# A fused per-channel scale and 384x384 matmul: reordering the first loads and splitting one weight copy

## The chip, the cores and the metric

The kernel runs on one core of one Trainium2 chip. The metric is the device time of one execution in microseconds (us); the median of three runs of the kernel before is 574.29 us (574.18 to 574.39). The core has a matrix engine (TensorE, PE in the profile; its weight loads have a row of their own, PEld), a vector engine (VectorE, DVE), a scalar engine (ScalarE, ACT), GpSimd (POOL) and SyncE (SP), which only issues DMAs and waits. SyncE and ScalarE each have a DMA queue of their own (q1 and q10 in the profile). The engines run independently and wait for each other through semaphores.

## The reference

```python
# x: (1, 384, 384, 384) bf16, dw: (1, 1, 384) bf16, pw: (384, 384) bf16
out = x * dw[0, 0][None, None, None, :]            # k = 1: the depthwise convolution is a scale per channel
return jnp.einsum('bhwc,cd->bhwd', out, pw)        # 147,456 rows of 384 times a 384 x 384 matrix
```

The scale can be moved into the matrix once, `w = dw[:, None] * pw`, and then the work is `x @ w`: 147,456 rows in 288 supertiles of 512 rows.

## The kernel before

TensorE contracts over partitions, but x arrives with its rows on partitions. VectorE therefore transposes x in 32x32 blocks of 32-bit words (pairs of bf16 channels), and TensorE works with contractions of 32 rows, four of them side by side in the array. The matrix must have the matching order of rows and copies in all four groups of 32 partitions. Making it is the *prologue*: TensorE multiplies a scaled selection matrix with pw into PSUM, six *pieces* `i = 2k + r` (k: 128 rows of pw, r: even or odd channels), and ScalarE or VectorE copies each piece from PSUM to `w_r`. Then the main loop runs: transposes on VectorE, 48 matmuls per supertile on TensorE, one PSUM copy per supertile on ScalarE, loads and stores by DMA.

The loads at the start (x0 and x1 are the first two chunks of x, of 384 KB each; x2 is 768 KB):

```python
w_eng = [1, 0, 1, 1, 1, 1]            # piece -> engine: 1 = ScalarE, 0 = VectorE
w_all = [(s_wr[e], w_eng.count(e)) for e in range(2)]      # what GpSimd awaits before its copy of w_r

nc.scalar.dma_start(dw_row[:], ...).then_inc(s_dw, 16)                  # L178
nc.sync.dma_start(pw_n[:, 0], pw[0:P, :]).then_inc(s_pw, 16)            # L179
nc.sync.dma_start(pw_n[:, 1:3], pw[P:C, :]....).then_inc(s_pw2, 16)     # L180
load_x(0)                                                               # L133, SyncE
# ... SyncE then issues x1, x2, x3, ... and later the stores
```

TensorE's prologue and the start of the main loop:

```python
w_first = {(0, 0): [(0, 1), (1, 3)], (4, 0): [(1, 4)], (4, 1): [(1, 5)]}   # step -> (engine, copies) awaited
steps = [(b, par) for b in range(4) for par in range(2)] + [(4, 0), (5, 0), (4, 1), (5, 1)]

idle_work(4)                     # L242: 4 x 4 matmuls of ones, results never read
nc.tensor.wait_ge(s_dw, 16)
...                              # L255: dw turned onto partitions by 3 matmuls
idle_work(2)                     # L242: 2 x 4 more
nc.tensor.wait_ge(s_pw, 16)
times = {(2, 0): 2, (2, 1): 2}   # these two pieces are computed twice (the same result)
for k in range(3):
    if k == 1:
        nc.tensor.wait_ge(s_pw2, 16)
    nc.tensor.wait_ge(s_sw, k + 1)                 # VectorE has scaled selection matrix k
    for r in range(2):
        if k == 2:
            nc.tensor.wait_ge(*w_done[r])          # the PSUM banks of piece r are free again
        for v in [0, 1] * times.get((k, r), 1):
            mm = nc.tensor.matmul(PS[(k + 1) % 2][:, 2 * r + v, :D], ...)   # L275
        mm.then_inc(s_w)
# main loop, first supertile, first step (b, par) = (0, 0): waits for s_t[0][0] (x0's first block is
# transposed) and for w_first[(0, 0)]; then 4 matmuls (L225), next step, ...
```

VectorE and ScalarE:

```python
def transposes(t, j):
    ...
    for h in range(2):
        if h == 0 and j == 0:
            nc.vector.wait_ge(sem, n)              # the chunk of x has landed
        if h == 0 and jj == 0:
            for b in range(3):                     # x0's first half in three blocks
                x_b = Xw[:, :, 0, 32 * b : 32 * b + 32]
                nc.vector.transpose(out=Tw[:, b], in_=x_b).then_inc(s_tb if b else s_t[0][0])   # L367
            continue
        ...                                        # L369: all other transposes, half a supertile each

def w_out(i):
    e, k, r = w_eng[i], i // 2, i % 2
    out, in_ = w_r[:, 2 * k : 2 * k + 2, r, :], w_ps(i)
    o = nc.vector.tensor_copy(out, in_) if e == 0 else nc.scalar.copy(out, in_)     # L385
    o._wait_ge(s_w, i + 1)
    o.then_inc(s_wr[e])
...
for i in range(6):
    w_out(i)
transposes(*order[0])        # x0
transposes(*order[1])        # x1
```

ScalarE executes, in this order: the DMA issue of dw, a table load (L341), two tiny copies (L341), its five pieces, and then one PSUM copy per supertile (L429).

Of the kernel before, what the change touches and what calls it, by code (L numbers as in the profile page):

```python
# [26 lines left out]
def kernel(  # L27
# [12 lines left out]
    nc = tc.nc  # L40
    P = nc.NUM_PARTITIONS
    B, H, W, C = x.shape
# [17 lines left out]
    NT = len(chunks)  # L60
# [13 lines left out]
    pw_n = raw[:, 0 : 3 * D].rearrange("p (k d) -> p k d", d=D)  # L74
# [29 lines left out]
    s_pw = nc.alloc_semaphore("s_pw")  # L104
    s_pw2 = nc.alloc_semaphore("s_pw2")
# [5 lines left out]
    s_wr = [nc.alloc_semaphore(f"s_wr{e}") for e in range(2)]  # L111

    with tc.tile_critical(sync_engine=mybir.EngineType.Pool, no_gpsimd_drain=True):
        def x_of(t):
            g, i, off, first, L = chunks[t]
            if first + 2 == NS:
                return Xl[:], s_xl, 32
            n = sum(len(ls) > i for ls in groups[g % NR : g + 1 : NR])
            return Xs[g % NR][:, 4 * off : 4 * (off + L), :], s_x[g % NR][i], 16 * n

        def load_x(t, eng=nc.sync):
            g, i, off, first, L = chunks[t]
            dst, sem, _ = x_of(t)
            rows = xf[512 * first : 512 * (first + L), :]
            if first + 3 < NS:
                src = rows.rearrange("(p s) c -> p (s c)", p=P)
                dst = dst.rearrange("p s c -> p (s c)")
                if i == 0 and g >= NR:
                    je = g_end[g - NR]
                    eng.wait_ge(s_t[je % 2][1], je // 2 + 1)  # L130
            else:
                src = rows.rearrange("(a k q) c -> q a k c", k=4, q=4)
            eng.dma_start(dst, src).then_inc(sem, 16)  # L133
# [39 lines left out]
            eng.dma_start(dst, src).then_inc(s_o[g % NR], 16)  # L173

        w_eng = [1, 0, 1, 1, 1, 1]
        w_all = [(s_wr[e], w_eng.count(e)) for e in range(2)]

        nc.scalar.dma_start(dw_row[:], dw.rearrange("a e c -> a (e c)")).then_inc(s_dw, 16)  # L178
        nc.sync.dma_start(pw_n[:, 0], pw[0:P, :]).then_inc(s_pw, 16)  # L179
        nc.sync.dma_start(pw_n[:, 1:3], pw[P:C, :].rearrange("(k p) d -> p k d", p=P)).then_inc(s_pw2, 16)  # L180
        load_x(0)

        todo = []
        for t, (g, i, off, first, L) in enumerate(chunks):
            if 0 < t < NT - 2:
                todo.append((g_end[g - NR] if g >= NR else -1, load_x, (t,)))
            for k in range(n_parts[t] - (first + 1 == NS)):
                todo.append((first + L * (k + 1) // n_parts[t] + 1, store, (t, k)))
# [15 lines left out]

        w_done = [(s_wr[e], w_eng[: i + 1].count(e)) for i, e in enumerate(w_eng)]

        w_first = {(0, 0): [(0, 1), (1, 3)], (4, 0): [(1, 4)], (4, 1): [(1, 5)]}

        def w_ps(i):
            return PS[0 if i in (2, 3) else 1][:, 2 * (i % 2) : 2 * (i % 2) + 2, :D]  # L210
# [28 lines left out]
        def idle_work(n):  # L239
            for _ in range(n):  # L240
                for i in range(4):
                    nc.tensor.matmul(  # L242
                        PS[0][:, 2 * (i % 2) + i // 2, :D],
                        lhsT=ones[32 * i : 32 * i + 32, 0:P],
                        rhs=ones[32 * i : 32 * i + 32, :],
                        start=True,
                        stop=True,
                        tile_position=(32 * i, 0),
                    )
# [10 lines left out]
                stop=True,  # L260
            )
        mm.then_inc(s_df)
        idle_work(2)
        nc.tensor.wait_ge(s_pw, 16)
        times = {(2, 0): 2, (2, 1): 2}
        for k in range(3):
            if k == 1:
                nc.tensor.wait_ge(s_pw2, 16)
            nc.tensor.wait_ge(s_sw, k + 1)
            for r in range(2):  # L270
                if k == 2:
                    nc.tensor.wait_ge(*w_done[r])

                for v in [0, 1] * times.get((k, r), 1):
                    mm = nc.tensor.matmul(  # L275
                        PS[(k + 1) % 2][:, 2 * r + v, :D],
                        lhsT=sel_w[64 * v : 64 * v + 64, k, r, :, :].rearrange("p q w -> p (q w)"),
                        rhs=pw_n[64 * v : 64 * v + 64, k, :],
                        start=True,
                        stop=True,  # L280
                        tile_position=(64 * v, 0),
                    )
                mm.then_inc(s_w)
# [22 lines left out]
        for m in range(4):  # L306
# [14 lines left out]
            out=eye[:],  # L321
            in_=ones[:, 0:P],
# [20 lines left out]
        def transposes(t, j):  # L343
            g, i, off, first, L = chunks[t]
            jj = first + j
            s = jj % 2
            if jj + 1 == NS:
                nc.vector.wait_ge(s_xk, 32)
                Tw = Ts[s][:].bitcast(U32).rearrange("p b (m w) -> p (b m) w", w=32)
                for v in range(2):  # L350
                    blocks = slice(12 * v, 12 * v + 12)
                    ins = nc.vector.transpose(out=Tw[:, blocks], in_=Xk[:, blocks].bitcast(U32))  # L352
                    ins._wait_ge(s_pe, 2 * (jj - 2) + v + 1)
                    ins.then_inc(s_t[s][v])
                return
            X, sem, n = x_of(t)
            Xw = X.bitcast(U32).rearrange("p (k l) c -> p k l c", l=L)
            Tw = Ts[s][:].bitcast(U32).rearrange(
                "p b (k i) -> p b k i" if t < 2 else "p b (i k) -> p b k i", k=4
            )  # L360
            for h in range(2):
                if h == 0 and j == 0:
                    nc.vector.wait_ge(sem, n)
                if h == 0 and jj == 0:
                    for b in range(3):
                        x_b = Xw[:, :, 0, 32 * b : 32 * b + 32]
                        nc.vector.transpose(out=Tw[:, b], in_=x_b).then_inc(s_tb if b else s_t[0][0])  # L367
                    continue
                ins = nc.vector.transpose(  # L369
                    out=Tw[:, 3 * h : 3 * h + 3],  # L370
                    in_=Xw[:, :, j, 96 * h : 96 * h + 96].rearrange("p k (b w) -> p b k w", w=32),
                )
                if jj >= 2:
                    ins._wait_ge(s_pe, 2 * (jj - 2) + h + 1)
                ins.then_inc(s_t[s][h])
# [3 lines left out]

        order = [(t, j) for t in range(NT) for j in range(chunks[t][4])]  # L380

        def w_out(i):
            e, k, r = w_eng[i], i // 2, i % 2
            out, in_ = w_r[:, 2 * k : 2 * k + 2, r, :], w_ps(i)
            o = nc.vector.tensor_copy(out, in_) if e == 0 else nc.scalar.copy(out, in_)  # L385
            o._wait_ge(s_w, i + 1)
            o.then_inc(s_wr[e])
# [3 lines left out]
            out=sel[:],  # L391
            in_=eye[:].rearrange("p (v w r) -> p r w v", v=2, r=2),
# [10 lines left out]
        for i in range(6):  # L403
            w_out(i)
        transposes(*order[0])
        transposes(*order[1])

        for jj, (t, j) in enumerate(order):
            g, i, off, first, L = chunks[t]
# [28 lines left out]
            if jj + 2 < NS:  # L438
                transposes(*order[jj + 2])
# [30 lines left out]
```

## Time and profile before

| what | value | where it is from |
|---|---|---|
| time, median of three | 574.29 us | the times |
| span of the profiled execution | 572.1 us | the page |
| TensorE busy | 567.4 us (99%) | the page, first part |
| VectorE / ScalarE busy | 508.4 us (89%) / 418.6 us (73%) | the page, first part |
| main-loop matmuls (L225) | 13776, in the chain from 6.31 to 566.55 us | chain of waits |
| first copy of a supertile on ScalarE starts | 8.91 us | timeline |
| moved by DMA | 226.88 MB, mean 397 GB/s | the page, second part |

The page is one execution, taken by the hardware profiler. A line of a group reads: line, engine, operation, what it writes and reads, count, then total busy time, mean duration of one in ns, and the idle time of the engine before such instructions with what ended it. Matmuls are pipelined: a duration is longer than the distance to the next one. The first thing to see in the table is that TensorE is occupied nearly from end to end, and that the whole prologue takes the first 6.3 us of 572.1.

### The profile page before, as it was taken

How to read it: one execution, taken by the hardware profiler on the slowest of the kernel's cores; microseconds unless marked ns; L12 is line 12 of the kernel's file. 1: busy time of each engine (PE TensorE's matmuls, PEld its weight loads, DVE VectorE, ACT ScalarE, POOL GpSimd, SP SyncE). 2: the span in 40 equal slices, each digit the busy share in tenths (PEclk: the TensorE clock that was granted, in tenths of full speed). 3: DMA queues.
4: the chain of work that ended last, by engine and by line, in shares of the span. 5: the costliest groups of instructions: out<-in, count | busy, mean ns of one | idle time of the engine just before them, and what ended most of it. 6: DMA issues, size and time to landing. Idle time of an engine off the chain costs nothing.

```text
span 572.1 us, 29707 instructions
## 1 busy us (share of the span) xinstructions
PE 567.4 (99%) x13843; PEld 354.3 (62%) x13843; DVE 508.4 (89%) x588; ACT 418.6 (73%) x298; POOL 13.9 (2%) x41
## 2 busy tenths in 40 slices
PE   9999999999999999999999999999999999999997
PEld 4666666666666666666666666666666666666664
DVE  6899999999999999999999999999999999999996
ACT  6777777777777777777777777777777777777775
POOL 2042000000000000000000000000000000000000
PEclk9999999999999999999999999999999999999999
DMA  8999999999999999999999999999999999997777
GB/s 328 445 395 411 423 416 430 442 417 417 426 413 423 383 398 438 385 387 399 433 380 388 414 415 402 408 405 415 408 395 433 395 391 403 423 389 313 327 287 263
DMA packets 26740, 226.88 MB, mean 397 GB/s; under 512 B 1385, under 2 KB 7274, under 8 KB 22890
## 3 DMA queue, kind: packets, MB, share of 16 engines
q1 hardware_dynamic: 25796, 225.91, 97.5%
q10 hardware_dynamic: 934, 0.89, 0.4%
q14 instruction: 9, 0.07, 0.0%
q8 instruction: 1, 0.02, 0.0%
HBM read 113.54 MB, written 113.25 MB: 396 GB/s over the span
## 4 chain that ended last, share of the span: by engine, by line
PE 99%; ACT 0%; issue 0%
PE ps L225 98%; PE ps L275 1%; PE ps L242 0%; PE ps L310 0%; PE ps L298 0%; ACT O L424 0%; PE ps L255 0%
## 5 line engine op out<-in xcount | busy, mean ns | idle before, releaser
L225 PE MATMUL ps<-w_r,T 32*128 32x384 bf16 x13776 | 560.3, 321 | 0.0
L369 DVE STREAM_TRANSPOSE T<-X 128x384 uint32<-128x384 uint32 x571 | 500.4, 879 | 54.8 <-DMA X<-in_x_dram 2.3
L429 ACT CAST O<-ps 128x1536 bf16<-128x1536 f32 x286 | 411.6, 1439 | 147.0 <-PE ps L225 147.0
L225 PEld LDWEIGHTS ps<-w_r,T 32*128 32x128 bf16 x13776 | 351.6, 93 | 209.0 <-issue 0.9
L339 POOL COPY Xk<-Xl 32x256 bf16<-32x256 bf16 x16 | 6.3, 394 | 0.0
L338 POOL COPY Xk<-Xl 32x128 bf16<-32x128 bf16 x16 | 4.6, 287 | 25.6 <-DMA Xl<-in_x_dram 24.7
L385 ACT CAST w_r<-ps 128x768 bf16<-128x768 f32 x5 | 3.6, 818 | 0.8 <-PE ps L275 0.8
L333 POOL COPY raw<-w_r 32x768 bf16<-32x768 bf16 x4 | 3.3, 819 | 6.4 <-ACT w_r L385 6.2
L242 PE MATMUL ps<-const-bfloat16-1.0 32*128 32x384 bf16 x24 | 2.2, 514 | 1.1 <-PEq L454 1.1
L275 PE MATMUL ps<-raw 64*128 64x384 bf16 x16 | 2.9, 513 | 0.1
L341 ACT ACT_TABLE_LOAD x1 | 1.3, 1283 | 1.5 <-PEq L454 1.5
L420 DVE CAST O<-ps 128x384 bf16<-128x384 f32 x2 | 1.0, 553 | 1.4 <-PE ps L225 1.4
L275 PEld LDWEIGHTS ps<-raw 64*128 64x128 bf16 x16 | 0.9, 114 | 2.2 <-DMA raw<-in_pw_dram 1.1
L369 DVE STREAM_TRANSPOSE T<-Xl 128x384 uint32<-128x384 uint32 x2 | 1.8, 882 | 0.2
L390 DVE TENSOR_REDUCE sel<-eye 128x64 f32<-128x128 bf16 x1 | 0.3, 289 | 1.5 <-POOL eye L320 1.5
L352 DVE STREAM_TRANSPOSE T<-Xk 128x384 uint32<-128x384 uint32 x2 | 1.2, 578 | 0.5 <-PE ps L225 0.4
L242 PEld LDWEIGHTS ps<-const-bfloat16-1.0 32*128 32x128 bf16 x24 | 0.7, 117 | 1.4 <-issue 1.4
L310 PE MATMUL ps<-raw,T 128*128 128x384 bf16 x8 | 1.5, 328 | 0.0
L424 ACT CAST O<-ps 128x384 bf16<-128x384 f32 x2 | 1.0, 479 | 0.7 <-PE ps L310 0.7
L385 DVE CAST w_r<-ps 128x768 bf16<-128x768 f32 x1 | 1.0, 957 | 0.5 <-PE ps L275 0.5
L367 DVE STREAM_TRANSPOSE T<-X 128x128 uint32<-128x128 uint32 x3 | 0.7, 284 | 0.6 <-DMA X<-in_x_dram 0.6
L424 DVE CAST O<-ps 128x384 bf16<-128x384 f32 x2 | 1.1, 558 | 0.1
(14 smaller groups left out, 5.3 us busy)
## 6 DMA issues: line engine op xcount, KB each, us to landing
X<-in_x_dram SPq DMA_DIRECT2D x26, 3840.0 KB, 21.7
out_dram<-O SPq DMA_DIRECT2D x26, 3840.0 KB, 27.6
X<-in_x_dram SPq DMA_DIRECT2D x3, 1536.0 KB, 18.4
out_dram<-O SPq DMA_DIRECT2D x4, 768.0 KB, 7.7
out_dram<-O SPq DMA_DIRECT2D x2, 1536.0 KB, 13.4
X<-in_x_dram SPq DMA_DIRECT2D x1, 2304.0 KB, 20.1
out_dram<-O SPq DMA_DIRECT2D x1, 2304.0 KB, 11.0
X<-in_x_dram SPq DMA_DIRECT2D x4, 384.0 KB, 4.4
```

The source lines that it names most:

```text
L225: mm = nc.tensor.matmul(PS[s][:, q, :D], lhsT=Ts[s][32 * q : 32 * q + 32, b, par::2], rhs=w_r[32 * q : 32 * q + 32, b, par, :], start=(b, ...
L242: nc.tensor.matmul(PS[0][:, 2 * (i % 2) + i // 2, :D], lhsT=ones[32 * i : 32 * i + 32, 0:P], rhs=ones[32 * i : 32 * i + 32, :], start=True ...
L275: mm = nc.tensor.matmul(PS[(k + 1) % 2][:, 2 * r + v, :D], lhsT=sel_w[64 * v : 64 * v + 64, k, r, :, :].rearrange("p q w -> p (q w)"), rhs ...
L310: mm = nc.tensor.matmul(PS[1][:, m, :D], lhsT=Tk[:, P * (m + 2) : P * (m + 3), par], rhs=w_k[:, par, :], start=False, stop=par == 1,)
L333: nc.gpsimd.tensor_copy(w_k[quads[n]], w_r[quads[n], n]).then_inc(s_wk)
L338: nc.gpsimd.tensor_copy(Xk[quads[n], g:8:4, :], x_b).then_inc(s_xk)
L339: nc.gpsimd.tensor_copy(Xk[quads[n], 8 + g : 24 : 4, :], Xl[quads[g], :, 64 * n : 64 * n + 64]).then_inc(s_xk)
L341: nc.scalar.copy(warm[:, s : s + 1], nc.const_aps.tensor(0.0, [P, 1], F32)).then_inc(s_a[s])
L369: ins = nc.vector.transpose(out=Tw[:, 3 * h : 3 * h + 3], in_=Xw[:, :, j, 96 * h : 96 * h + 96].rearrange("p k (b w) -> p b k w", w=32),)
L385: o = nc.vector.tensor_copy(out, in_) if e == 0 else nc.scalar.copy(out, in_)
L424: o = (nc.scalar.copy if n % 2 else nc.vector.tensor_copy)(Ov[:, n, j, :], PS[s][:, n, :D])
L429: a = nc.scalar.copy(Ov[:, :, j, :], PS[s][:, :, :D])
```

## The change

It rearranges the first six microseconds. SyncE now loads the first 256 rows of pw in one DMA, then x0, then x2 and so on; ScalarE's queue loads dw, the last 128 rows of pw, and x1. Piece 3 (`k = 1, r = 1`) is copied out of PSUM by both engines: ScalarE takes its first PSUM bank (384 columns), VectorE the second, and VectorE's half stands between the first and the second transposed block of x0. The waits are adapted: the first main step needs two VectorE copies instead of one, and pw's second semaphore is awaited before k = 2 instead of k = 1. The filler work of TensorE moves too: three groups of `idle_work` instead of two before the pieces, and piece 3 is computed twice instead of pieces 4 and 5. Its purpose is to have x0 and the first four pieces ready earlier, so that the main loop can begin earlier.

```diff
-        w_all = [(s_wr[e], w_eng.count(e)) for e in range(2)]
+        w_all = [(s_wr[0], 2), (s_wr[1], 5)]

         nc.scalar.dma_start(dw_row[:], dw.rearrange("a e c -> a (e c)")).then_inc(s_dw, 16)
-        nc.sync.dma_start(pw_n[:, 0], pw[0:P, :]).then_inc(s_pw, 16)
-        nc.sync.dma_start(pw_n[:, 1:3], pw[P:C, :].rearrange("(k p) d -> p k d", p=P)).then_inc(s_pw2, 16)
+        nc.sync.dma_start(pw_n[:, 0:2], pw[0 : 2 * P, :].rearrange("(k p) d -> p k d", p=P)).then_inc(s_pw, 16)
         load_x(0)
+        nc.scalar.dma_start(pw_n[:, 2], pw[2 * P : C, :]).then_inc(s_pw2, 16)
+        load_x(1, nc.scalar)
...
-            if 0 < t < NT - 2:
+            if 1 < t < NT - 2:
...
-        w_first = {(0, 0): [(0, 1), (1, 3)], (4, 0): [(1, 4)], (4, 1): [(1, 5)]}
+        w_first = {(0, 0): [(0, 2), (1, 3)], (4, 0): [(1, 4)], (4, 1): [(1, 5)]}
...
-        idle_work(2)
+        idle_work(3)
         nc.tensor.wait_ge(s_pw, 16)
-        times = {(2, 0): 2, (2, 1): 2}
+        times = {(1, 1): 2}
         for k in range(3):
-            if k == 1:
+            if k == 2:
                 nc.tensor.wait_ge(s_pw2, 16)
...
                         nc.vector.transpose(out=Tw[:, b], in_=x_b).then_inc(s_tb if b else s_t[0][0])
+                        if b == 0:
+                            w_out(3, 1)
...
-        def w_out(i):
+        def w_out(i, bank=0):
             e, k, r = w_eng[i], i // 2, i % 2
             out, in_ = w_r[:, 2 * k : 2 * k + 2, r, :], w_ps(i)
+            if i == 3:
+                out, in_ = out[:, bank], in_[:, bank]
+                e = 1 - bank
```

## The prediction, made before the changed kernel was run

> **What bounds the kernel now.** I read the page's first part, then the chain of waits, then the timelines of TensorE, ScalarE and VectorE for the first 9 us. The page's busy times:
>
> ```profile
> PE 567.4 (99%) x13843; PEld 354.3 (62%) x13843; DVE 508.4 (89%) x588; ACT 418.6 (73%) x298; POOL 13.9 (2%) x41
> ```
>
> The chain of waits in order of time (start, length, what):
>
> ```profile
> 0.80 0.32 issue
> 1.12 1.49 PE ps L242 x15
> ...
> 3.36 1.47 PE ps L275 x8
> 4.83 0.02 issue
> 4.85 1.47 PE ps L275 x8
> 6.31 560.24 PE ps L225 x13175
> 566.55 0.65 PE ps L298 x16
> ```
>
> The reader is to see that TensorE is the chain, and that L225 runs in one piece for 560.24 us without a wait. Nothing the change touches lies inside that piece. So the change can act in one way only: by the moment at which the main loop starts, and by the speed at which its first matmuls run. Everything after, the tail included (some 5.5 us from 566.55 to the span's end at 572.1), shifts with it.
>
> What ends last before the main loop is in the timelines of ScalarE and VectorE (start, length, operation, and in brackets the idle time before it and its releaser):
>
> ```profile
> 3.91 3.61 ACT L385 CAST w_r<-ps 128x768 bf16<-128x768 f32 x5 [0.79 <-PE ps L275]
> ```
>
> ```profile
> 4.23 0.96 DVE L385 CAST w_r<-ps 128x768 bf16<-128x768 f32 x1 [0.48 <-PE ps L275]
> 5.83 0.70 DVE L367 STREAM_TRANSPOSE T<-X 128x128 uint32<-128x128 uint32 x3 [0.65 <-DMA X<-in_x_dram]
> 6.45 1.45 DVE L369 STREAM_TRANSPOSE T<-X 128x384 uint32<-128x384 uint32 x3
> ```
>
> The trace's single instructions refine this. ScalarE's pieces start at 3.906, 4.602, 5.292, 5.983 and 6.674 us, so 0.69 us apart, and the third (piece 3) reports at 6.12. x0's sixteenth and last completion comes at 5.80, the first transposed block starts at 5.83 and reports at 6.15. TensorE passes its wait at 6.15 and its first main matmul starts at 6.253. Two things end within 0.03 us of each other: the copy of piece 3, and x0. Only shortening both helps.
>
> Second observation: the clock. The same shape takes very different times on the page,
>
> ```profile
> L225 PE MATMUL ps<-w_r,T 32*128 32x384 bf16 x13776 | 560.3, 321 | 0.0
> ...
> L242 PE MATMUL ps<-const-bfloat16-1.0 32*128 32x384 bf16 x24 | 2.2, 514 | 1.1 <-PEq L454 1.1
> ```
>
> that is 321 ns in the loop and 514 in the filler. Groups of four start 0.320 us apart up to 7.18 us (6.542, 6.862, 7.182) and 0.1625 us apart from 7.39 on. The trace's clock record goes to full at 7.253. Between 6.253 and 7.253 the main loop ran at half speed, which cost it 0.5 us.
>
> [...] the record shows full clock at 7.253 and half again at 573.866, 566.61 us apart[...].
> [...] ScalarE's Xl load, issued at 24.51 us, has its packets spread from 28.0 to past 32.4 among SyncE's.
> [...]
>
> **The change, part by part.**
> *Loads.* An issue takes SyncE 0.39 to 0.46 us. x0's issue moves from third to second place, from 1.87 to about 1.41 us: 0.46 earlier. But the DMA engines were already moving pw without a hole: packets of 768 bytes (36 ns each) from 1.97 to about 3.45, then x0's from 3.21 on. Before x0 could finish, 288 KB of pw and 384 KB of x0 had to pass; that remains. New is that x1, issued by ScalarE at about 2.0 (after dw, 0.54 us, and pw's rest, 0.42), has packets ready about 0.6 us after its issue ends, near 3.1, and takes turns with x0. Two estimates for x0's landing: if the slow first packets (up to 1.3 us instead of 121 ns) overlap between the queues, x0 is through at 4.9 and lands 0.3 us later, at 5.2 to 5.3; if the engines simply alternate, it is through at 5.7 and lands at about 6.0 to 6.2. I choose 5.6 us, against 5.80 before.
> pw's first 256 rows: sixteen packets per engine instead of eight, 0.29 us later than 2.84, so 3.13. TensorE waited for the scaled selection until 3.23 anyway, so the first piece stays at 3.36.
> *ScalarE.* Two more issues push the table load from 1.54 to about 2.43; it and the tiny copies then end so that piece 0 can start at about 3.93 instead of 3.906. 0.02 us, nearly nothing. Pieces 0 and 2 take 0.69 each; half of piece 3 is a 128x384 copy, 479 ns by the page's row of that shape in the tail. It starts at 5.31 and reports at 5.81 instead of 6.12: 0.31 gained. Pieces 4 and 5 follow some 0.3 earlier and aren't awaited.
> *VectorE.* Piece 1 ends at 5.18 as before. Then x0's first block, which holds the engine for 0.24 us (5.828 to 6.064 between its starts), then the half copy: 558 ns by the same tail shape, then the semaphore. So the loop's wait ends at x0's landing + 0.03 + 0.24 + 0.56 + 0.02 = landing + 0.85, where before it was landing + 0.35. The half copy has been put behind x0 on the path. With landing at 5.60 the wait ends at 6.45, and the first matmul starts 0.10 later, at 6.55: 0.30 later than before. With landing under 5.15 the floor is 6.03, from piece 1's end.
> *TensorE's filler.* One more idle group fills 3.02 to 3.34, which was empty. Piece 3 done twice fills 4.60 to 4.92, mostly empty before. Without doubling, pieces 4 and 5 end at 5.56 instead of 6.11. So TensorE is busy from 1.12 to 5.56 without a hole, and then idle until 6.55, 1.0 us.
>
> **What this makes of the clock.** In the window 0.43 to 3.84, TensorE was busy 1.90 + 0.48 of 3.41 us (70%) and the clock was not released. After the change it is 2.72 (80%). In the window 3.84 to 7.253 it was busy 0.77 + 1.26 + 1.00 (89%), and it was released. After, it would be 1.72 + 0.70 (71%). [...] each of three ways is open:
> A, [...] the loop runs at full speed from 6.55. Before, it had done by 7.253 what full speed does in half of that 1.0 us, as though it had begun at 6.75 at full speed. So -0.20: 574.1.
> B, the clock still comes at 7.253: a start 0.30 later costs half of that, +0.15: 574.4.
> C, [...] the clock comes at 10.67, +0.15 and half of 3.41 more, +1.85: 576.1.
>
> **Rivals.**
> First: x0 arrives earlier by its whole issue gain, 5.34. Then the wait ends at 6.19, near the 6.15 of before, and only the clock decides: in A -0.46, in B +0.02. For it speaks that x0's first packets were slow for reasons that two queues may hide; against it the shared engines.
> Second: x1's interleaving takes x0 to 6.1: start at 7.05, in A +0.30, in B +0.40. C becomes likelier, as the hole grows to 1.5 us.
> Third: the loop is starved later, since x2 moves up and x1 over. VectorE waited for x2 0.82 us (until 8.72) without delaying TensorE: its result was awaited only at about 10.8, and reported at 9.61 and 10.33. With the same bytes in the same time I expect nothing of this.
> Fourth: a busier DMA or engine through the rest. No instruction there changes; it would be zero.
>
> **Range and chances.** I give A 0.5, B 0.2 and C 0.3. A with the uncertainty of x0 spans 573.8 to 574.6, B 574.3 to 574.7, C 575.9 to 576.3; runs of before differ by 0.2. The middle of the mixture is 574.3. The range that should hold it 8 times in 10 is 573.7 to 576.2; the upper side is long because of C. Two per cent are 11.5 us, more than the whole prologue, so faster 0.004, same 0.99, slower 0.006.
>
> **What would show it.** x0's wait on VectorE ending at 5.6; ScalarE's half copy of about 0.48 us ending at 5.8; a half copy of about 0.56 us on VectorE after the first block; the first L225 near 6.55; and the spacing of its groups: 0.16 from the start (A), from 7.25 (B) or only from 10.67 (C). The L225 piece of the chain should be 559.7 us in A, about 560.1 in B, 561.8 in C. I am wrong if x0 lands before 5.2 or after 6.2, if the clock comes at other times than these windows, or if the loop shows waits further on.

## The result and the profile after

The changed kernel takes 576.24 us (median of 6; 575.75 to 578.37) where the kernel before takes 574.23 (median of 6; 573.91 to 574.39). The medians differ by 2.0 us, a third of a per cent; the ratio of the means is 1.0044, 95% interval 1.0027 to 1.0061. All ratios below are of means, to the kernel before on the same chip. The prediction was 574.3 with a range to 576.2; the result lies just above the range. The six executions fall in two groups, four from 575.75 to 576.43 and two at 577.69 and 578.37. The profile below is of the one at 577.69; a second profile, at 576.31, follows among the experiments (e12).

First part of the page of the changed kernel, busy times:

```profile
PE 568.0 (99%) x13845; PEld 409.3 (71%) x13845; DVE 508.5 (88%) x589; ACT 417.9 (73%) x298; POOL 13.9 (2%) x41
```

TensorE's busy time has hardly moved. The loss is idle time, and the chain of waits says where:

```profile
1.94 8.15 DMA X<-in_x_dram
10.09 0.02 issue
10.12 0.59 DVE T L372
10.71 0.14 issue
10.84 559.56 PE ps L226 x13728
570.40 0.65 PE ps L299 x16
```

Before, the chain was TensorE throughout. Now it runs for 8.15 us along one load of x, issued at 1.94: that is x1, on ScalarE's queue. Its sixteen completions come between 6.80 and 10.09 us; before, between 6.09 and 6.73. VectorE transposes its first half, and only then does TensorE go on. From there the rest is as long as it was: 13,728 matmuls are 286 supertiles, one less than the loop's 287.

TensorE's timeline (start, length, then in brackets the idle time and what ended it):

```profile
3.60 1.27 PE L276 MATMUL ps<-raw 64*128 64x384 bf16 x10
5.54 0.50 PE L276 MATMUL ps<-raw 64*128 64x384 bf16 x4 [0.68 <-DMA raw<-in_pw_dram]
6.71 2.13 PE L226 MATMUL ps<-w_r,T 32*128 32x384 bf16 x48 [0.67 <-DVE w_r L391]
10.84 3.56 PE L226 MATMUL ps<-w_r,T 32*128 32x384 bf16 x44 [2.00 <-DVE T L372]
```

The first supertile (x48) runs at 6.71, then there is nothing until 10.84. VectorE and ScalarE in the same stretch:

```profile
5.70 0.31 DVE L368 STREAM_TRANSPOSE T<-X 128x128 uint32<-128x128 uint32 x1 [0.32 <-DMA X<-in_x_dram]
5.94 0.52 DVE L391 CAST w_r<-ps 128x384 bf16<-128x384 f32 x1
6.38 0.48 DVE L368 STREAM_TRANSPOSE T<-X 128x128 uint32<-128x128 uint32 x2
6.79 0.53 DVE L372 STREAM_TRANSPOSE T<-X 128x384 uint32<-128x384 uint32 x1
10.12 2.46 DVE L372 STREAM_TRANSPOSE T<-X 128x384 uint32<-128x384 uint32 x4 [2.79 <-DMA X<-in_x_dram]
```

```profile
4.14 3.29 ACT L391 CAST w_r<-ps 128x768 bf16<-128x768 f32 x5 [0.15 <-PE ps L276]
```

x0's first block starts at 5.70, the half copy follows it, and after x0 VectorE waits 2.79 us for x1. The hole also costs something afterwards. Busy times by stretch (columns: stretch, length, then PE, PEld, DVE, ACT and POOL busy, PEclk, DMA share, GB/s):

```profile
9.00:10.00 1.00, 0.00 (x0) 0.00 (x0) 0.00 (x0) 1.00 (x1) 0.94 (x2) 1.00 1.11 461
10.00:11.00 1.00, 0.16 (x4) 0.15 (x8) 0.88 (x2) 0.33 (x1) 0.94 (x2) 1.00 1.06 449
11.00:12.00 1.00, 1.00 (x20) 0.62 (x16) 1.00 (x3) 0.00 (x0) 0.03 (x1) 0.52 0.95 406
13.00:14.00 1.00, 1.00 (x20) 0.62 (x16) 0.70 (x1) 0.00 (x0) 0.00 (x0) 0.50 1.22 522
14.00:15.00 1.00, 1.00 (x28) 0.62 (x23) 0.30 (x1) 0.30 (x1) 0.00 (x0) 0.77 1.02 428
```

The granted clock (PEclk) falls to one half at 11.04 us and comes back at 14.45, 3.41 us later; the trace's clock record has both moments.

**The sum.** The last matmul starts 3.85 us later than before. The loop starts 0.46 later (6.71 instead of 6.25). The clock was full from 4.21 on, so the 0.50 us that the cold start cost before is saved. The hole is 2.32 us between two matmul starts, less the usual 0.16: 2.16. The 3.41 us at half speed cost half of that, 1.71, for groups of four matmuls start 0.320 us apart there and 0.1625 before and after. 0.46 - 0.50 + 2.16 + 1.71 = 3.83 (3.82 before rounding). Without the fall of the clock it is 2.12. The same four terms (start of the loop, cold start, holes, fall of the clock) are given for every profile in a table below.

### The profile page after: what moved, and what is told of

It is laid out like the page before. It is cut to its first block, busy times and chain, and to the rows that moved or that the text cites. A ratio compares the mean times of both kernels' runs of the same rounds, so it can differ in the third digit from the quotient of the medians.

```text
span 576.0 us, 29711 instructions
## 1 busy us (share of the span) xinstructions
PE 568.0 (99%) x13845; PEld 409.3 (71%) x13845; DVE 508.5 (88%) x589; ACT 417.9 (73%) x298; POOL 13.9 (2%) x41
## 4 chain that ended last, share of the span: by engine, by line
PE 98%; DMA 1%; ACTq 0%; DVE 0%; issue 0%; ACT 0%; POOLq 0%
PE ps L226 97%; DMA X<-in_x_dram 1%; PE ps L311 0%; PE ps L299 0%; DVE T L372 0%; ACTq L178 0%; ACT O L430 0%; ACTq L181 0%; ACTq L471 0%; POOLq L113 0%; POOLq L460 0%
## 5 line engine op out<-in xcount | busy, mean ns | idle before, releaser
L226 PEld LDWEIGHTS ps<-w_r,T 32*128 32x128 bf16 x13776 | 406.6, 93 | 157.8 <-issue 3.4
L391 ACT CAST w_r<-ps 128x768 bf16<-128x768 f32 (+1 forms) x5 | 3.3, 745 | 0.2 <-PE ps L276 0.2
L391 DVE CAST w_r<-ps 128x768 bf16<-128x768 f32 (+1 forms) x2 | 1.5, 738 | 0.7 <-PE ps L276 0.7
```

The source lines that it names most:

```text
L226: mm = nc.tensor.matmul(PS[s][:, q, :D], lhsT=Ts[s][32 * q : 32 * q + 32, b, par::2], rhs=w_r[32 * q : 32 * q + 32, b, par, :], start=(b, ...
```

## The experiments

Theory 1, from the changed kernel's trace: the packets of x1 (3 KB, ScalarE's queue) and of x2 (6 KB, SyncE's queue) take turns, so x1 gets the smaller share of the bytes. By 8.00 us 103 of x1's packets had started and 97 of x2's. Theory 2: the split copy, which starts the loop later, and the holes in TensorE's work before it.

**e1: x1 back on SyncE, the rest as changed.**

```diff
-        load_x(1, nc.scalar)
-            if 1 < t < NT - 2:
+            if 0 < t < NT - 2:
```

> The changed kernel with x1 loaded by SyncE again, between x0 and x2; ScalarE's queue keeps dw and the last third of pw; split, waits and filler as changed. Theory 1 (x1's packets of 3 KB on ScalarE's queue alternate one for one with x2's of 6 KB on SyncE's, so x1 lands at 10.1 us and the second supertile waits 2.0 us): x1 lands before 7, no hole after the first supertile, 574.2 to 574.6. Theory 2 (the split copy, which sets the loop's start to 6.71 us, and the holes in TensorE's work before it are the cost): the start stays near 6.7 and some 1 to 2 us stay lost, 575.2 to 576.

Measured: 574.28 us (573.85 to 575.97, 12 runs), ratio 1.0004 (0.9993 to 1.0016). x1 lands at 7.65. TensorE's timeline:

```profile
3.57 2.57 PE L275 MATMUL ps<-raw 64*128 64x384 bf16 x14
6.88 5.38 PE L225 MATMUL ps<-w_r,T 32*128 32x384 bf16 x128 [0.74 <-ACT w_r L390]
```

The loop starts even later than in the changed kernel, at 6.88, and then has no hole. The two microseconds hang on this one line; theory 2 as the main cost falls.

**e2: the kernel before, with x1 alone moved to ScalarE's queue.**

```diff
         load_x(0)
+        load_x(1, nc.scalar)
-            if 0 < t < NT - 2:
+            if 1 < t < NT - 2:
```

> The kernel before, with nothing changed but x1's issue, which goes to ScalarE's queue after dw. Theory 1: this alone makes the loss; x1 lands near 9 to 10 us, the second supertile waits 1 to 2.5 us, 575.5 to 577. Theory 2: 574.2 to 574.5, as the copies and the filler are those of before.

Measured: 576.40 us (4 runs), ratio 1.0045 (1.0028 to 1.0062). The time is as theory 1 has it, the way is not: x1 landed ahead of x0, at 5.59. The victims were the loads that stood on SyncE's queue with smaller packets or behind them: pw's last 256 rows (768-byte packets) came at 5.61 instead of 3.83, x0 at 6.54 instead of 5.80.

```profile
5.66 2.10 PE L276 MATMUL ps<-raw 64*128 64x384 bf16 x12 [1.47 <-DMA raw<-in_pw_dram]
7.85 4.38 PE L226 MATMUL ps<-w_r,T 32*128 32x384 bf16 x88
```

Pieces 2 to 5 wait for pw, and the loop starts at 7.85. So the loads with the smaller packets lost here, not the one on ScalarE's queue.

**e3: as changed, but SyncE issues x2 only after x1 has landed.**

```diff
+            if f is load_x and a == (2,):
+                nc.sync.wait_ge(x_of(1)[1], 16)
             f(*a)
```

> The changed kernel, but SyncE issues x2 only when x1 has landed; x1 stays on ScalarE's queue. Theory 1: x1 lands near 6, the second supertile does not wait; x2 then lands near 9.5, in time for the third supertile at about 10.7, or just late; 574.2 to 575. Rival 1b (a load from ScalarE's queue is late whatever stands beside it): x1 still lands after 8 us and x2 later still, 577 or more.

Measured: 575.56 us (7 runs), ratio 1.0026 (1.0015 to 1.0038). x1 landed at 6.22 on ScalarE's queue, with x2 not yet issued, so rival 1b falls. But x2 now came at 10.38 (expected 9.5), and VectorE waited for it instead:

```profile
10.48 4.37 DVE L374 STREAM_TRANSPOSE T<-X 128x384 uint32<-128x384 uint32 x6 [2.12 <-DMA X<-in_x_dram]
```

TensorE lost 0.70 us there before the third supertile, and another 0.55 at 26.9 us, in a hole for which the profile shows no wait.

**e4: as changed, x2 in two DMAs with 3 KB packets.**

```diff
+            if t == 2:
+                for h in range(2):
+                    part = slice(4 * C * h, 4 * C * h + 4 * C)
+                    eng.dma_start(dst[:, part], src[:, part]).then_inc(sem, 16)
+                return
             eng.dma_start(dst, src).then_inc(sem, 16)
```

> The changed kernel with x2 (the same bytes) loaded as two DMAs with packets of 3 KB instead of one with 6 KB; x1 stays on ScalarE's queue. Theory 1 in its packet form: the two queues now take equal shares of bytes, so x1 is through when two times 384 KB have passed instead of three times; it lands near 8.6 instead of 10.1, and the second supertile waits about 0.7 us instead of 2.0: 574.8 to 575.3. Rival 1c (the DMA engines' low rate of 216 to 304 GB/s from 4 to 7 us is the cause, and shares don't matter): x1 lands at 10 as before, 576 or more.

**e9: as changed, x1 in two DMAs with 1.5 KB packets** (the same edit for `t == 1`, with half the slice; the waits for this semaphore count 16 more).

> The changed kernel with x1 (the same bytes, still on ScalarE's queue) loaded as two DMAs with packets of 1.5 KB instead of one with 3 KB. If the queues take turns packet by packet, x1's sixteen packets on each DMA engine must now sit out eight of x2 (6 KB, 0.23 us) and then eight of x3 (12 KB, 0.46 us) instead of eight of x2: x1 lands near 13 us instead of 10.1, the second supertile waits 4 to 6 us, 579 to 582. If shares go by bytes or time, or a second queue is merely slow at the start, x1 lands at 10 to 10.6 and the time is 576 to 577 (a second issue on ScalarE adds 0.4 us before its first copy).

Measured: e4 574.94 us (20 runs), ratio 1.0017 (1.0010 to 1.0024), x1 lands at 9.05. e9 577.79 (4 runs), ratio 1.0065 (1.0050 to 1.0080), x1 lands at 11.72. The chains of waits, e4 first:

```profile
1.93 7.12 DMA X<-in_x_dram
9.05 0.02 issue
9.08 0.59 DVE T L378
9.67 0.14 issue
9.80 557.88 PE ps L231 x13728
```

```profile
2.41 9.31 DMA X<-in_x_dram
11.72 0.02 issue
11.74 0.59 DVE T L377
12.33 0.14 issue
12.47 559.56 PE ps L231 x13728
```

The same bytes, and x1 lands at 9.05, 10.09 and 11.72. These three distances alone are not a proof, for a second profile of the changed kernel (e12 below) has x1 at 8.84 with unchanged packets. What holds in every one of these profiles is the company in which x1 lands. As changed, x1 and x2 have eight packets each on every DMA engine, and they land together (10.09 and 10.41; in e12 8.84 and 9.08). In e9 x1 has sixteen and lands with x3 (11.72 and 11.95). In e4 x2 has sixteen, and x1 lands 1.02 us ahead of it (9.05 and 10.07). Before, on one queue, x1 came 1.89 us ahead of x2 (6.73 and 8.62). The packet counts say the same: by 8.00 us of the changed kernel's profile 103 packets of x1 and 97 of x2 have started, of 128 each; by 9.00 us of e9's profile 209 of x1 and 192 of x2 and x3, of 256 each, though the latter are four times as large. So in these two profiles the loads side by side were served nearly alike in packets and not in bytes: some 309 KB of x1 beside 582 of x2, 314 of x1 beside 1152 of x2 and x3.

How late x1 comes in us depends on a second thing, the pace of the DMA. Stretches of the changed kernel's profile, then the same of e12:

```profile
5.00:6.00 1.00, 0.46 (x4) 0.11 (x4) 0.68 (x3) 1.00 (x3) 0.00 (x0) 1.00 0.74 225
6.00:7.00 1.00, 0.33 (x10) 0.27 (x12) 1.00 (x5) 1.00 (x3) 0.00 (x0) 1.00 0.93 304
```

```profile
5.00:6.00 1.00, 0.33 (x4) 0.00 (x0) 0.37 (x1) 0.97 (x2) 0.00 (x0) 1.00 1.05 409
6.00:7.00 1.00, 0.82 (x4) 0.13 (x4) 0.63 (x2) 0.29 (x1) 0.00 (x0) 1.00 1.02 412
```

(PEclk reads 1.00 ahead of the first clock record, at 4.21 and 10.36 us, though until 4.21 the first profile has groups of matmuls 0.320 us apart, as at half clock.) In the first profile single packets of x1 took up to 1.4 us, and 216 to 316 GB/s were moved from 4 to 8 us, against 383 to 418 in e12. The slow pace, rival 1c of e4, is not the whole cause: e4 had it too (200, 237, 307 GB/s from 4 to 7 us), and its x1 came 1.04 us sooner. An estimate by theory 1 from the usual durations of a packet in the traces, 0.234 us for a 6 KB packet, 0.121 for 3 KB, 0.065 for 1.5 KB: e4 saves 8 x (0.234 - 0.121) = 0.90 us, e9 adds 16 x (0.065 + 0.234) - 8 x (0.121 + 0.234) = 1.94. Measured from 10.09 it was 1.04 and 1.63; measured from e12's 8.84 it would miss by about a microsecond. My expectation for e9 was too high because it gave x3 packets of 12 KB; they have 6 KB. In time e4 (ratio 1.0010 to 1.0024) is clear of the changed kernel (1.0027 to 1.0061); e9 (1.0050 to 1.0080) is not.

**e8: the other way round, x0 alone on ScalarE's queue,** pw in three DMAs of 128 rows on SyncE's, VectorE's half of piece 3 ahead of x0's first block.

```diff
-        nc.sync.dma_start(pw_n[:, 1:3], pw[P:C, :]....).then_inc(s_pw2, 16)
-        load_x(0)
+        nc.sync.dma_start(pw_n[:, 1], pw[P : 2 * P, :]).then_inc(s_pw2, 16)
+        nc.sync.dma_start(pw_n[:, 2], pw[2 * P : C, :]).then_inc(s_pw3, 16)
+        load_x(0, nc.scalar)
```

> A version meant to use the packet alternation: x0 (3 KB packets) alone on ScalarE's queue after dw, pw in three DMAs of 128 rows and then x1, x2 on SyncE's; piece 3 split with VectorE's half ahead of x0; filler as before. If queues take turns packet by packet, x0's packets gain over pw's 768-byte ones: x0 lands near 4.9 instead of 5.80, pw's last rows later, near 4.5; start near 6.1, 573.7 to 574.1. If shares are by bytes or time, x0 lands at 5.6 or later and the time is 574.1 or more.

Measured: 575.69 us (7 runs), ratio 1.0034 (1.0021 to 1.0047). x0 landed at 5.24, but pw's second 128 rows, issued at 1.41, only at 5.04:

```profile
5.09 2.10 PE L279 MATMUL ps<-raw 64*128 64x384 bf16 x12 [0.90 <-DMA raw<-in_pw_dram]
7.13 5.19 PE L227 MATMUL ps<-w_r,T 32*128 32x384 bf16 x80
```

A load of 96 KB in 768-byte packets took 3.6 us beside 3 KB packets. I had seen who would gain and not who would pay.

**e5: the kernel before with the split alone. e7: with the filler alone.**

```diff
# in part
# e5: w_all, w_first, w_out and the half copy after x0's first block as in the change
# e7:
-        idle_work(2)
+        idle_work(3)
-        times = {(2, 0): 2, (2, 1): 2}
+        times = {(1, 1): 2}
```

> The kernel before with the split of piece 3 alone (VectorE's half after x0's first block), loads and filler as before. If the split delays the loop as I worked out, the wait ends 0.85 us after x0's landing instead of 0.35, and TensorE starts some 0.25 later, near 6.9 instead of 6.25 us: 0.3 to 0.65 more, 574.4 to 574.8. If it is hidden (the rival: ScalarE's piece 3 was the later one and is now shorter), 573.9 to 574.2.

> The kernel before with TensorE's filler alone as changed (three idle groups, piece 3 twice, pieces 4 and 5 once). It computes the same. If the filler's place matters through the clock, [...] the spread changes: 573.6 to 575. If not, 573.9 to 574.3 and the start stays at 6.25 us.

Measured: e5 573.98 us (13 runs) against 573.98 of before on the same chip, ratio 1.0006 (0.9998 to 1.0015); e7 574.05 (13 runs), ratio 1.0008 (0.9998 to 1.0018). Neither makes a difference that these runs can tell. e5's chain shows the split on the path all the same:

```profile
1.87 3.44 DMA X<-in_x_dram
5.32 0.02 issue
5.34 0.31 DVE T L367
5.65 0.45 DVE w_r L390
6.11 0.24 issue
6.35 559.85 PE ps L225 x13776
```

From x0's landing to the first matmul are 1.03 us where I had worked out 0.95. But x0 landed at 5.32 here, not 5.80 as in the profile of before, so the start is 6.35. In the five profiles with the loads of before (before, e5, e7, e10, e11) x0 lands between 5.32 and 5.80, which hides such a term. e7's profile shows a cost of the filler: the third idle group puts TensorE's first piece at 3.55 instead of 3.36, though pw's first rows were there at 2.93, and ScalarE starts its copies later than the 3.91 of before:

```profile
4.09 0.80 ACT L385 CAST w_r<-ps 128x768 bf16<-128x768 f32 x1 [0.98 <-PE ps L275]
```

Its loop starts at 6.44.

**e6: e1 with VectorE's half ahead of x0's first block. e10 and e11: attempts to beat both.** e10 is the kernel before with three idle groups and pieces 3, 4 and 5 done twice; e11 has the loads of before, the split with VectorE's half first, and three idle groups.

```diff
# in part
# e6, e11:
         for i in range(6):
             w_out(i)
+        w_out(3, 1)
         transposes(*order[0])
```

> The run with x1 back on SyncE, with VectorE's half of piece 3 moved from behind x0's first block to ahead of it. The loop's wait should then end at the later of x0's landing + 0.35 and the half's report near 5.95: a start near 6.3 instead of 6.88, so 0.3 to 0.5 less than that run's 574.28: 573.8 to 574.0. If the split isn't on the path, no difference.

> The kernel before with all of TensorE's holes filled: three idle groups, and pieces 3, 4 and 5 each computed twice. If a fuller window brings the full clock earlier and takes away late-clock executions (about one in ten of the kernel before lies above 575), the median falls by 0.1 to 0.3 and nothing lies above 575: 573.7 to 573.9. If the doubled pieces delay the loop instead: 574.1 to 574.4.

> A version meant to beat both: loads of the kernel before (all on SyncE but dw), piece 3 split with VectorE's half ahead of x0's first block, three idle groups, pieces 4 and 5 twice. ScalarE's part of piece 3 is done near 5.8, VectorE's near 5.75, x0's first block at its landing + 0.35; with x0 at 5.3 to 5.8 the loop starts at 6.1 to 6.3 instead of 6.25 to 6.4: 573.7 to 574.0. If pieces 4 and 5 (done twice up to 6.1) set the start, no gain: 573.9 to 574.1.

Measured: e6 574.09 us (13 runs), ratio 1.0006 (0.9997 to 1.0015); e10 574.24 (21 runs), ratio 1.0007 (1.0000 to 1.0013); e11 574.04 (13 runs, from 573.37), ratio 1.0003 (0.9993 to 1.0013). In e11's profile the loop starts at 6.15, the earliest of all, but nothing here is shown to beat the kernel before. Three of e10's executions lie above 575, where none was expected. e6's profile is of an execution at 575.81: pw's last rows landed at 5.88 and the full clock came at 10.05.

**e12: the changed kernel once more, for a second profile.**

> The changed kernel once more, for a second profile of it. Theory: x1 again lands at 9 to 10.5 us and the second supertile waits about 2 us; where the clock does not fall back afterwards the time is 575.8 to 576.4, where it does (one window of 3.41 us at half speed), 577.5 to 578.4.

Measured: 576.31 us (5 runs, 574.71 to 578.61), ratio 1.0042 (1.0021 to 1.0064). The profile, of an execution at 576.31, loses by another way:

```profile
1.47 4.88 DMA X<-in_x_dram
6.35 0.02 issue
6.37 0.31 DVE T L368
6.68 0.46 DVE w_r L391
7.14 0.24 issue
7.38 561.27 PE ps L226 x13775
```

This time x0 landed at 6.35 and pw's rest at 6.12. TensorE idled before the loop, started at 7.38, and the full clock came only at 10.36, so that the loop ran 2.98 us at half speed. x1 came at 8.84, and with the slow first supertile that was early enough: no hole. The expected hole of 2 us was not there, the expected time was: the late start and the late clock make +2.12, as much as the first profile's hole without the fall of the clock. So the times cannot tell which of the two ways the other executions near 576 took.

**All profiles in four terms** (us; each taken from the trace's single instructions and its clock record, each from one execution, which need not be like the median; "sum" and "measured" are differences from the kernel before, the latter by the start of the last matmul):

| kernel | loop starts | full clock from | cold cost | holes | fall of clock | sum | measured |
|---|---|---|---|---|---|---|---|
| before | 6.25 | 7.25 | 0.50 | 0 | 0 | 0 | 0 |
| after | 6.71 | 4.21 | 0 | 2.16 | 1.71 | +3.82 | +3.85 |
| e12, after again | 7.38 | 10.36 | 1.49 | 0 | 0 | +2.12 | +2.10 |
| e1 | 6.88 | 6.28 | 0 | 0 | 0 | +0.13 | +0.16 |
| e2 | 7.85 | 9.17 | 0.66 | 0 | 0 | +1.76 | +1.75 |
| e3 | 6.82 | 5.25 | 0 | 1.25 | 0 | +1.32 | +1.40 |
| e4 | 6.34 | 6.90 | 0.28 | 1.24 | 0 | +1.11 | +1.13 |
| e5 | 6.35 | 5.48 | 0 | 0 | 0 | -0.41 | -0.36 |
| e6 | 6.68 | 10.05 | 1.68 | 0 | 0 | +1.61 | +1.59 |
| e7 | 6.44 | 5.43 | 0 | 0.30 | 0 | -0.01 | +0.04 |
| e8 | 7.13 | 10.75 | 1.81 | 0 | 0 | +2.18 | +2.16 |
| e9 | 6.88 | 6.18 | 0 | 3.62 | 1.71 | +5.45 | +5.48 |
| e10 | 6.44 | 4.03 | 0 | 0 | 0 | -0.31 | -0.28 |
| e11 | 6.15 | 4.41 | 0 | 0.40 | 0 | -0.19 | -0.14 |

Cold cost is half the time from the loop's start to the full clock. The sums hold within 0.08 us, so no fifth cause is needed; past 28 us nothing in the loop has changed.

## Why the prediction was wrong

**What held.** Almost all of the loop is untouched, and the change acts within the first 15 us. The halves took 498 ns on ScalarE and 520 on VectorE (479 and 558), VectorE's half did stand on the path, and in the first profile x0 landed at 5.68 (5.6 predicted) and the first matmul came at 6.71 (6.55). The extra filler group did close the hole at 3.02. Of the three ways of the clock two were seen: A in the first profile and C in the second. That C's numbers came out so close, 10.36 us against 10.67 and 576.31 against 576.1, is in part luck: the loop started 0.83 us later than predicted, and the slow clock cost 0.57 less. It is luck, too, that the median lies so near the range: its upper end stood for C, and the middle was 574.3.

**The step that failed** in the first profile is the third rival, the later chunks: "With the same bytes in the same time I expect nothing of this." I let x1 compete with x0 and asked only when x0 would come; x1's own landing I never worked out. Beside x2's packets, at a slow pace of the DMA (216 to 316 GB/s from 4 to 8 us), it landed at 10.09 instead of 6.73. TensorE wanted x1's first half, transposed, at 8.7, so x1 itself by about 7.9 (the transposes and the start take 0.75 us from x1's landing). It also made my case A too good: an early clock brings the first supertile forward, and then x1's lateness is bare; at e12's landing of 8.84 the hole would still be about 0.9 us, by estimate. In the second profile the step that failed is the landing of x0, which I chose at 5.6: it came at 6.35, later than my second rival's 6.1, and the start at 7.38 met a late clock. e1 shows that x1's place on ScalarE's queue is worth the whole loss: of 25 executions of e1 and e6, with x1 back on SyncE, five lie above 575.5, of the eleven of the changed kernel nine. By which of the two ways it costs most executions their 2 us is not shown.

**A second step failed, in the place of the clock.** A, B and C take the full clock's moment from one profile: 7.253 us, or about 3.41 to either side. That distance was my assumption when I wrote them; the changed kernel's record has it once, from 11.04 to 14.45. That the moment stays where it is was an assumption too, from a few close times and one profile, and it was wrong: in fourteen profiles the full clock starts at fourteen different times between 4.03 and 10.75 us, and the changed kernel alone has 4.21 and 10.36. So A and C are not alternatives of which one holds: the same kernel showed an early clock in one execution and a late one in another.

**Terms mis-sized.** Piece 0 was to stay at 3.36, its copy at 3.93; the copy came at 4.14 (4.09 in e12). Most of this is the third idle group, which holds piece 0 back to 3.55 in e7, e10, e11 and e12 alike; pw's 256 rows, at 3.55 instead of 3.13 (3.27 in e12), add 0.05 in the first profile. pw's last 128 rows, 768-byte packets beside x0's, landed at 5.50 and 6.12; I had pieces 4 and 5 finished by 5.56, and they began at 5.54 and 6.16. x0 itself came at 6.35 in the second profile, outside my 5.2 to 6.2. The new order of loads has no visible gain: in the seven profiles that issue x0 second on SyncE it landed between 5.08 and 6.35, against 5.32 to 5.80 with the loads of before, and pw's last rows between 4.36 and 6.12, against 3.83 to 4.22.

**What stays open.** Why some executions deliver x0 late (5.68 or 6.35 in the same kernel), and why the pace of the DMA from 4 to 8 us differs, was not tried. In e12 fifteen of x0's sixteen completions were there by 5.60 and the last came at 6.35: one straggler set the landing. That a fallen clock accounts for the two executions near 578 is shown for the profiled one; of the other, only its mean clock of 0.996 speaks for it. The short holes near 26 us in e3, e7 and e11 have no visible cause.

## What to carry to other kernels

Moving a load to a second queue brought no gain here: it changed which load came late, x1 at 10.09 us instead of 6.73 in the changed kernel, pw's last 256 rows at 5.61 instead of 3.83 in e2, and each of these two had the smaller packets (3 KB beside 6 KB, 768 bytes beside 3 KB). Before splitting loads over queues, list the packet sizes that will stand beside each other, and work out the landing of every load, not only of the one the change is for. When a change of a microsecond acts at the start, first see what the clock does there: in two profiles of the changed kernel the full clock came at 4.21 and 10.36 us, and the second lost 1.49 us by it.

## What the runs showed of the hardware

*The full clock and TensorE's work before it.* In the kernel before, TensorE was at work for 89% of the 3.41 us that end with the full clock at 7.253, and for 70% of the 3.41 us ahead of them (the prediction's counts; 3.41 us is the length of the stretch at half clock in the changed kernel). In the changed kernel it was at work for 83% of the 3.41 us that end with the full clock at 4.21. Whether this share decides is not shown.

*The clock's fall.* In the changed kernel the clock was full from 4.21 to 11.04 us; TensorE had worked 51% of the first half of that and 37% of the second when it fell. In e9 it fell after 58% and 16%. The holes of 2.16 us (after) and 3.62 us (e9) were each followed by a fall that cost 1.71 more, the holes of 1.24 us in e4 and 1.25 us in e3 by none.

*Packets of two loads side by side.* 103 packets of 3 KB had started beside 97 of 6 KB by 8.00 us (after), 209 of 1.5 KB beside 192 of 6 KB by 9.00 us (e9). The same counts do not give the landing: x1 landed at 10.09 and 8.84 us in two executions of one kernel, and the pace of the DMA differed between them (225 or 409 GB/s from 5 to 6 us).
